# Funnel attention and gated FFN on one core: one beam search for the order of all visits, and column-tile groups of two pairs

## The chip, the cores and the metric

The kernel runs on one core of one Trainium2 chip. The metric is the device time of one execution in microseconds (us); the time of a kernel is the median of several runs.

## The reference

Attention with pooled queries, followed by a multiplicative FFN. All heads have 64 dimensions; 8 batches, 8 heads, 1152 keys, 576 pooled queries.

```python
q_pool = q.reshape(B, H, S // 2, 2, D).mean(axis=3)          # 8, 8, 576, 64
scores = 1 / sqrt(D) * q_pool @ k.T                          # 8, 8, 576, 1152
attn = softmax(scores)
attn_out = attn @ v                                          # 8, 8, 576, 64
x = attn_out.transpose(0, 2, 1, 3).reshape(4608, 512)
a, b = x @ w1, x @ w2                                        # 4608, 1024
out = ((a * b) @ w3) @ w_out                                 # 4608, 512
```

## The kernel before

**Pairs, slots and visits.** Two heads are one pair (32 pairs, `NP`). For a pair, the 9 key tiles times 576 queries are one flat row of 5184 score columns, and the rows of all pairs follow one another. They are cut into 324 slots of 512 columns. A slot is a few matmuls (`scores`, L396, 64 rows of the array for each of the two heads) into one of three PSUM tiles `psc`, and one exponential on ScalarE (L401) into a ring `ring` in SBUF that holds 2.67 pairs. Three slots make a visit; there are 108 visits. A pair is 3.375 visits long.

**What stands between the scores.** After its three slots, a visit has a string of steps in an order that a planner writes down while the program is built:

- `A`, an AV group (`av_step`): attention weights times values for 128 queries of a pair, 18 matmuls (L426) over the 9 key tiles and two heads. A pair has four such tiles and one of the last 64 queries. There the two heads go to two column halves of the array (L423, 18 matmuls too, called `C` in this text). All write into one PSUM bank, `avb`. A ones column in the values gives the sums; VectorE takes the reciprocal (L452, L446), scales (L460, L448) and so makes `xbt` or `xb5`. Its transpose is done in the next `A` by one matmul on PE (`T`: L467, or L469 for the 64 queries) with a copy on VectorE (L476, L478); for pairs from 8 on (`XD`) the four 128-query tiles go by one DMA transpose instead (`x_dma`, L436, SyncE's queue).
- `f` and other filler steps (`fill`): products of w3 and w_out early on (turnings of w3 L496, products L505), then the FFN in chunks of 512 tokens: 16 projections (L527, 4 matmuls) and 4 output steps (L571, 8 matmuls, called `F`). A filler uses the single bank `mo`, or borrows a `psc` bank (the tile is then `mot`).
- `P`: transposes of keys and queries of pairs 1 to 7 on PE into a `psc` bank (`transp_pe`, L336). From pair 8 on a DMA transpose makes `kqT` (L328, SyncE's queue).

PE has three tilings: 64 rows by 128 columns for scores, 128 by 64 for `C`, 128 by 128 for all the rest.

**The planner.** `_Plan` keeps running times of PE, ScalarE, VectorE, the three `psc` banks, `mo` and `avb`. For each visit on its own, `visit` tries all strings of up to six steps, adds the next three slots, and takes the string of least cost: PE time lost, plus 0.2 x the distance from a set pace (`PACE` = 3.09 us a visit, kept in `due`), plus a price for a late `avb`, less a bonus for AV groups done. A chunk of the FFN comes into the queue when its AV groups are done, and, where its `x` comes by DMA, `HELD` = 5 groups later. After the last visit the remaining AV groups and steps alternate (the tail).

**Queues.** SyncE's queue carries, in program order, the loads of k, q and v, the `kqT` transposes and `x_dma`; GpSimd's queue carries the casts to 16 bits, early loads, and the stores of outputs from three `osb` buffers (L539). `prepare` issues casts and loads two pairs ahead.

Of the kernel before, what the change touches and what calls it, by code (L numbers as in the profile page):

```python
# [121 lines left out]
class _Plan:  # L122
# [3 lines left out]
    SWITCH, SLOT, AV, LAST, TURN, PAIR, SEEN = 0.09, 0.222, 0.553, 0.36, 0.055, 0.76, 0.05  # L126
    STEP = {0.5: 0.45, 1: 0.866, 2: 1.73}

    def __init__(self, t):
        self.t = t  # L130
        self.act = self.mo = self.av = self.dve = 0.0
        self.psc = [0.0, 0.0, 0.0]
        self.k = 0
        self.mode = "row"

    def _pe(self, mode, free, took):
        if mode != self.mode:
            self.t += self.SWITCH
            self.mode = mode
        self.t = max(self.t, free) + took  # L140
# [5 lines left out]
    def scores(self):  # L146
        b = self._psc()
        self._pe("row", self.psc[b] + self.SEEN, self.SLOT)
        self.act = max(self.act, self.t + 0.21) + 0.953
        self.psc[b] = self.act + 0.07  # L150

    def fill(self, n, at, scored):
        b = self._psc() if scored else None
        self._pe("full", max(at, (self.psc[b] if scored else self.mo) + self.SEEN), self.STEP[n])
        self.dve = max(self.dve, self.t + 0.2) + 0.69
        if scored:
            self.psc[b] = self.dve + 0.07
        else:
            self.mo = self.dve + 0.07

    def av_group(self, turns, last):
        if last:
            self._pe("col", self.av + self.SEEN, self.LAST)
        else:
            self._pe("full", self.av + self.SEEN, self.AV)
        if turns:
            self._pe("full", 0.0, self.TURN)
        self.dve = max(self.dve, self.t + 0.2) + 0.49 + (0.21 if turns else 0.0)
        self.av = self.dve + 0.02

    def pair(self, at):
        b = self._psc()
        self._pe("full", max(at, self.psc[b] + self.SEEN), self.PAIR)
        self.dve = max(self.dve, self.t + 0.1) + 0.9
        self.psc[b] = self.dve + 0.07

    def copy(self):
        p = _Plan(self.t)
        p.__dict__.update(self.__dict__)
        p.psc = list(self.psc)  # L180
        return p

    def visit(self, due, turns, must, groups, pair_at, eager):


        best = [None, None]

        def end(p, seq, work, av):
            q = p.copy()
            for _ in range(3):  # L190
                q.scores()
            lost = q.t - self.t - work - 3 * self.SLOT
            cost = lost + 0.2 * abs(p.t - due) + 0.3 * max(q.av + self.SEEN - q.t, 0.0)
            cost -= eager * min(len(turns), 6) * av
            if best[0] is None or cost < best[0] - 1e-9:
                best[:] = [cost, seq]

        def step(p, seq, work, av, f, pr):
            if pr == len(pair_at) and av >= must:
                end(p, seq, work, av)  # L200
            if len(seq) > 5 or p.t > due + 0.5 and av >= must:
                return
            if pr < len(pair_at):
                q = p.copy()
                q.pair(pair_at[pr])
                step(q, seq + "P", work + self.PAIR, av, f, pr + 1)
            if av < min(len(turns), 3):
                q = p.copy()
                q.av_group(*turns[av])
                took = (self.LAST if turns[av][1] else self.AV) + (self.TURN if turns[av][0] else 0.0)  # L210
                step(q, seq + "A", work + took, av + 1, f, pr)
            if f < min(len(groups), 4):
                n, at = groups[f]
                for b in (False, True):
                    q = p.copy()
                    q.fill(n, at, b)
                    step(q, seq + "ms"[b], work + self.STEP[n], av, f + 1, pr)

        step(self, "", 0.0, 0, 0, 0)
        return best[1]  # L220


@with_exitstack
def kernel(
# [11 lines left out]
    nc = tc.nc  # L236
# [21 lines left out]
    NU = NP * NT5  # L258
# [23 lines left out]
    xps = avb[:, 448:448 + QT]  # L282
# [131 lines left out]
    def av_pair(i):  # L414
        p, t = i // NT5, i % NT5
        va = vaugs[p % NVA]
        o = (i % 3) * 2 * E1
        for jt in range(NJ):
            c0 = ((p * NJ + jt) * Sq) % RING + TO[t]
            for u in range(2):  # L420
                if t == QM:

                    nc.tensor.matmul(avb[u * QT:u * QT + QT, o:o + E1], ring[:, u, c0:c0 + QT], va[:, u, jt, :],  # L423
                                     start=(jt == 0), stop=(jt == NJ - 1), skip_group_check=True)
                    continue
                nc.tensor.matmul(avb[:, o + u * E1:o + u * E1 + E1], ring[:, u, c0:c0 + 128], va[:, u, jt, :],  # L426
                                 start=(jt == 0 and u == 0), stop=(jt == NJ - 1), skip_group_check=True)
# [11 lines left out]
    def on_pe(i):  # L439
        return i >= 0 and (i // NT5 < XD or i % NT5 == QM)  # L440

    def av_norm(i):
        o = (i % 3) * 2 * E1
        if i % NT5 == QM:

            nc.vector.reciprocal(out=rzall[:, i, :], in_=avb[:, o + D:o + E1].to_broadcast([128, 2]))  # L446
            xbts[i] = att.tile([128, 2, D], FP16, tag="xbt", bufs=3, name="xbt")
            nc.vector.scalar_tensor_tensor(out=xbts[i], in0=avb[:, o:o + D].unsqueeze(1).to_broadcast([128, 2, D]),  # L448
                                           scalar=rzall[:, i, 0:1], in1=half, op0=ALU.mult, op1=ALU.mult)
            return  # L450
        av = avb[:, o:o + 2 * E1].rearrange("p (u e) -> p u e", e=E1)
        nc.vector.reciprocal(out=rzall[:, i, :], in_=av[:, :, D:E1].rearrange("p u o -> p (u o)"))  # L452
        p, t = i // NT5, i % NT5
        if i // NT5 < XD:
# [9 lines left out]
    def x_turn(i):  # L464
        xb = xbts.pop(i).rearrange("p u d -> p (u d)")
        if i % NT5 < QM:
            nc.tensor.transpose(xpt, xb, ident16)  # L467
        else:
            nc.tensor.matmul(xps, xb, both, start=True, stop=True, skip_group_check=True)  # L469

    def x_copy(i):
        p, t = i // NT5, i % NT5
# [4 lines left out]
        else:  # L477
            nc.vector.tensor_copy(out=xT[:, hp, c0:c0 + QT], in_=xps)  # L478
# [133 lines left out]
    def fill(scored=False):  # L612
# [3 lines left out]
        if not tail[0]:  # L616
            plan.fill(n, at, scored)
# [58 lines left out]
    pair_end = [((p + 1) * FLAT - 1) // G // VS for p in range(NP)]  # L676
    done_at = {}
    for c in range(B * Sq // CH):
        last = max((b * HP + HP - 1) * NT5 + t for b in range(B) for t in range(NT5)
                   if xpos(b, t) < (c + 1) * CH and xpos(b, t) + (128 if t < QM else QT) > c * CH)  # L680
        done_at.setdefault(last, []).append(c)

    final.extend(done_at[max(done_at)])
    plan = _Plan(7.0)
    PACE = 3.09
    W3_AT, WO_AT, KQ_AT = (17.5, 28.0, 35.0, 44.0), 20.5, {2: 24.5}
    avn = [0]
    ready, held = [], []
    HELD = 5

    def av_step():
        i = avn[0]
        avn[0] += 1
        av_pair(i)
# [5 lines left out]
        if i >= XD * NT5 and i % NT5 == QM - 1:  # L700
            x_dma(i // NT5)
        if i:
            for c in done_at.get(i - 1, []):
                held.append((i + (HELD if i > XD * NT5 else 0), c))
        while held and held[0][0] <= i:
            ready.append(held.pop(0)[1])

    NVIS = NS // VS
    seen, due, started = -1, 0.0, False
    for vis in range(NVIS):  # L710
        if vis == T_START:
            queue.append(t_groups())
        due = max(due + PACE, plan.t + 2.6)
        for s in range(vis * VS, vis * VS + VS):
# [13 lines left out]
            plan.scores()  # L728
# [5 lines left out]
        avail = NT5 * sum(1 for e in pair_end if e < vis) - avn[0]  # L734
        turn = [p for p in range(1, NPE) if (p * FLAT // G) // VS - 1 == vis]
        while ready:
            started = True
            queue.append(moe_groups(ready.pop(0)))
        head(4)

        must = sum(1 for i in range(avn[0], min(avn[0] + avail, NU))
                   if ((i // NT5 * NJ * Sq + RING + TO[i % NT5]) // G) // VS <= vis + 1)
        for what in plan.visit(due, [(on_pe(avn[0] + j - 1), (avn[0] + j) % NT5 == QM) for j in range(avail)], must, [(g[0], g[3]) for g in ahead],
                               [KQ_AT.get(p, 0.0) for p in turn], 0.05 if started else 0.1):
            if what == "P":
                plan.pair(KQ_AT.get(turn[0], 0.0))
                transp_pe(turn.pop(0))
            elif what == "A":
                av_step()
                plan.av_group(on_pe(avn[0] - 2), (avn[0] - 1) % NT5 == QM)  # L750
            else:
                fill(what == "s")
    fill(True)
    while avn[0] < NU:
        av_step()
        while ready:
            queue.append(moe_groups(ready.pop(0)))
        fill(True)
    tail[0] = True
    x_turn(NU - 1)  # L760
    x_copy(NU - 1)
    ready.extend([c for _, c in held] + done_at.get(NU - 1, []))
    while ready:
        queue.append(moe_groups(ready.pop(0)))
# [57 lines left out]
```

## Time and profile before

| | us |
|---|---|
| median of 3 runs | 420.6 (419.92 to 420.74) |
| profiled execution, time | 421.74 |
| profiled execution, span | 419.7 |
| PE busy | 404.0 |
| ScalarE (ACT) busy | 325.8 |
| VectorE (DVE) busy | 207.1 |
| scores from / tail from | 7.13 / 345.6 |

The span runs from the first to the last instruction; the time of an execution has 2.04 us more around it. The granted PE clock is 0.997 on the mean. Matmuls overlap in the pipeline and their ends are modelled, so distances between starts say more than bars.

### The profile page before, as it was taken

What the parts mean: (1) busy time and instruction counts of PE and PEld (TensorE: products, weight loads), DVE (VectorE), ACT (ScalarE), POOL (GpSimd) and SP (SyncE); (2) the same over time, 40 slices, a digit from 0 to 9 for tenths busy, and PEclk for the clock granted to TensorE, in tenths of its full rate; (3) what the DMA queues carried; (4) which work ended last, traced back from release to release, by engine and by line L of the source; (5) the groups of instructions that cost most, each with busy time, mean ns of one, the idle gap of its engine ahead of it and who ended that gap; (6) DMA issues with size and microseconds to landing.
All of it is one profiled execution on the core that took longest, in us unless ns stands there. A gap on an engine that the chain in (4) does not pass through costs nothing.

```text
span 419.7 us, 12781 instructions
## 1 busy us (share of the span) xinstructions
PE 404.0 (96%) x5337; PEld 246.6 (59%) x5337; DVE 207.1 (49%) x601; ACT 325.8 (78%) x359; POOL 166.8 (40%) x210
## 2 busy tenths in 40 slices
PE   3899999999999999999999999999999999999995
PEld 1577886555566655655566556565577755444442
DVE  1255665664445534555455534555354546624231
ACT  4888879889999898989899889998999882223231
POOL 5879876360751427412564428141652011000000
PEclk9999999999999999999999999999999999999998
DMA  8999999999795999989989999899995323020203
GB/s 261 264 299 287 254 299 318 321 240 261 160 262 140 256 265 247 279 175 256 329 202 246 266 244 280 167 258 274 256 235 117 59 64 64 14 101 2 100 0 106
DMA packets 90960, 86.34 MB, mean 206 GB/s; under 512 B 59664, under 2 KB 64272, under 8 KB 90896
## 3 DMA queue, kind: packets, MB, share of 16 engines
q1 hardware_dynamic: 81600, 59.32, 59.7%
q0 software_dynamic: 8720, 25.10, 20.8%
q10 hardware_dynamic: 576, 1.05, 0.7%
q8 instruction: 42, 0.69, 0.7%
q14 instruction: 22, 0.18, 0.2%
HBM read 67.11 MB, written 9.44 MB: 182 GB/s over the span
## 4 chain that ended last, share of the span: by engine, by line
PE 89%; ACT 4%; DMA 3%; DVE 2%; issue 1%; POOL 0%; ACTq 0%; DVEq 0%
PE psc L396 19%; PE avb L426 17%; PE mot L527 16%; PE mo L527 14%; PE mo L571 9%; PE mot L571 5%; ACT ring L401 3%; PE mo L505 3%; PE avb L423 3%; DMA out_dram<-osb 2%; PE ptk L336 2%; DMA qst<-in_q_dram 1%; PE mo L496 1%; PE avb L467 1%; DVE kqT L338 1%
## 5 line engine op out<-in xcount | busy, mean ns | idle before, releaser
L401 ACT ACTIVATE ring<-psc 128x1024 f16<-128x1024 f32 x324 | 307.5, 1026 | 34.4 <-PE psc L396 33.4
L396 PE MATMUL psc<-kqT 64*128 64x512 f16 (+7 forms) x1152 | 97.9, 292 | 3.4 <-ACT ring L401 0.9
L426 PEld LDWEIGHTS <-ring 128*128 128x128 f16 x2304 | 83.2, 98 | 27.2 <-issue 8.5
L426 PE MATMUL avb<-vaug,ring 128*128 128x65 f16 x2304 | 91.5, 194 | 1.1 <-DVE xT L478 0.9
L308 POOL CAST kq<-kst 128x1152 f16<-128x1152 f32 x31 | 35.7, 1151 | 79.3 <-DMA kqT<-kq 64.7
L396 PEld LDWEIGHTS <-kqT 64*128 64x128 f16 x1152 | 46.1, 95 | 34.9 <-issue 12.7
L571 PE MATMUL mo<-T,gT 128*128 128x512 f16 x192 | 45.5, 380 | 0.0
L527 PEld LDWEIGHTS <-w2sb 128*128 128x128 f16 x320 | 28.0, 97 | 27.4 <-issue 3.7
L571 PEld LDWEIGHTS <-gT 128*128 128x128 f16 x280 | 25.5, 98 | 30.6 <-issue 3.1
L527 PEld LDWEIGHTS <-w1sb 128*128 128x128 f16 x320 | 28.1, 97 | 25.6 <-issue 1.8
L539 POOL DMA_DIRECT2D out_dram<-osb x21 | 11.7, 555 | 76.3 <-DVE osb L581 41.1
L452 DVE RECIPROCAL rzall<-avb 128x2 f32<-128x2 f32 x128 | 21.1, 165 | 41.5 <-PE avb L426 22.4
L527 PE MATMUL mot<-xT,w1sb 128*128 128x512 f16 (+2 forms) x176 | 41.1, 360 | 0.0
L312 POOL TENSOR_TENSOR kq<-qst 128x512 f16<-128x512 f32 x31 | 39.4, 1272 | 1.3 <-DMA qst<-in_q_dram 1.3
L321 POOL CAST vaug<-vst 128x1152 f16<-128x1152 f32 x32 | 36.6, 1143 | 8.3 <-DMA vst<-in_v_dram 8.2
L560 DVE TENSOR_TENSOR gT<-mo,asb 128x512 f16<-128x512 f32 x36 | 24.9, 692 | 25.9 <-PE mo L527 25.9
L527 PE MATMUL mo<-xT,w2sb 128*128 128x512 f16 (+2 forms) x176 | 37.2, 341 | 0.0
L527 PE MATMUL mot<-xT,w2sb 128*128 128x512 f16 x144 | 37.0, 379 | 0.2 <-ACT ring L401 0.2
L581 DVE TENSOR_SCALAR osb<-mo 128x512 f32<-128x512 f32 x24 | 16.6, 692 | 41.1 <-PE mo L571 38.0
L560 DVE TENSOR_TENSOR gT<-mot,asb 128x512 f16<-128x512 f32 x36 | 24.9, 692 | 23.3 <-PE mot L527 23.3
L554 ACT COPY asb<-mot 128x512 f32<-128x512 f32 x20 | 11.7, 585 | 31.2 <-PE mot L527 31.2
L527 PE MATMUL mo<-xT,w1sb 128*128 128x512 f16 (+2 forms) x144 | 33.0, 356 | 0.0
(76 smaller groups left out, 314.9 us busy)
## 6 DMA issues: line engine op xcount, KB each, us to landing
vst<-in_v_dram SPq DMA_DIRECT2D x25, 576.0 KB, 5.1
kst<-in_k_dram SPq DMA_DIRECT2D x23, 576.0 KB, 5.9
qst<-in_q_dram SPq DMA_DIRECT2D x23, 512.0 KB, 7.7
out_dram<-osb POOLq DMA_DIRECT2D x21, 256.0 KB, 6.1
kst<-in_k_dram POOLq DMA_DIRECT2D x8, 576.0 KB, 9.1
qst<-in_q_dram POOLq DMA_DIRECT2D x8, 512.0 KB, 10.0
vst<-in_v_dram POOLq DMA_DIRECT2D x7, 576.0 KB, 7.5
out_dram<-osb SPq DMA_DIRECT2D x9, 256.0 KB, 2.1
```

The lines of the kernel that those rows point to most:

```text
L308: nc.gpsimd.tensor_copy(out=kq16[:, 0:NJ].rearrange("p c u d -> p u c d"), in_=kst.rearrange("p u (c d) -> p u c d", d=D))
L312: eng.tensor_tensor(out=kq16[:, NJ:NJ + QM].rearrange("p c u d -> p u c d"), in0=qv[:, :, :, 0], in1=qv[:, :, :, 1], op=ALU.add)
L321: nc.gpsimd.tensor_copy(out=va[:, :, :, 0:D], in_=vs.pop(p).rearrange("p u (c d) -> p u c d", d=D))
L396: nc.tensor.matmul(psc[:, u, f - s * G:f - s * G + ln], kT2[u * 64:u * 64 + 64, jt, :], qpT[u * 64:u * 64 + 64, i0:i0 + ln], start=True, s ...
L401: nc.scalar.activation(out=ring[:, :, r0:r0 + G], in_=psc, func=AF.Exp, bias=0.0, scale=SCALE)
L423: nc.tensor.matmul(avb[u * QT:u * QT + QT, o:o + E1], ring[:, u, c0:c0 + QT], va[:, u, jt, :], start=(jt == 0), stop=(jt == NJ - 1), skip_ ...
L426: nc.tensor.matmul(avb[:, o + u * E1:o + u * E1 + E1], ring[:, u, c0:c0 + 128], va[:, u, jt, :], start=(jt == 0 and u == 0), stop=(jt == N ...
L452: nc.vector.reciprocal(out=rzall[:, i, :], in_=av[:, :, D:E1].rearrange("p u o -> p (u o)"))
L527: nc.tensor.matmul(pw[:, d0:d0 + n], wt[:, mc, ft * 128:ft * 128 + 128], xT[:, mc, a:a + n], start=(mc == 0 and d0 == 0), stop=(mc == NC - ...
L560: nc.vector.tensor_tensor(out=t["g"][:, ft, :], in0=pb, in1=t["a"], op=ALU.mult)
L571: nc.tensor.matmul(po, t["g"][:, ft, tt:tt + 128], T16[:, ft, :], start=(ft == 0), stop=(ft == NF - 1))
L581: nc.vector.tensor_scalar_mul(out=osb, in0=po, scalar1=1.0 / (SCL * SCL))
```

## The change

One function, `_visits`, plans all visits before any is recorded. It keeps a beam of plans for each count of AV groups and filler steps done (`width` = 3 for each, none more than `REACH` = 1.5 worse than the best), extends each by all strings of up to five steps or 2.3 us, and returns the strings of the plan that loses least PE time at the end. There is no pace and no bonus. Some prices of `_Plan` are set anew, and its waits for `psc`, `mo` and `avb` include `SEEN`.

The 64-query groups of two pairs become one group of 36 matmuls with two results side by side in `avb`, one reciprocal, two scalings, two matmuls for the transposes and one copy. The order of AV groups becomes: four tiles of an even pair, the common 64-query group, four tiles of the odd pair (`UNITS`; 144 groups instead of 160). `avb` has two result slots instead of three. A chunk is released four groups (`HELD` = 4) after the last group whose DMA transpose it reads. The last group of all is now a 128-query group of pair 31.

```diff
-    SWITCH, SLOT, AV, LAST, TURN, PAIR, SEEN = 0.09, 0.222, 0.553, 0.36, 0.055, 0.76, 0.05
+    SWITCH, SLOT, AV, LAST, TURN, PAIR, SEEN = 0.097, 0.222, 0.556, 0.285, 0.057, 0.77, 0.05
...
-    def visit(self, due, turns, must, groups, pair_at, eager):
...
+def _visits(n, start, units, pairs, fills, free, ready, width):
+    p = _Plan(7.0)
+    for _ in range(3):
+        p.scores(0.0)
+    beam = {(0, 0): [p]}
+    for vis in range(n):
...
+        def end(p, seq, na, f):
+            q = p.copy()
+            for _ in range(3 if vis + 1 < n else 0):
+                q.scores(ready[vis + 1])
+            q.past = (p.past, seq)
+            cost = q.lost() + 0.3 * max(q.av - q.t, 0.0) + 0.15 * max(q.mo - q.t, 0.0)
+            new.setdefault((na, f), []).append((cost, seq, q))
...
+        floor = min(x[0] for v in new.values() for x in v)
+        beam = {}
+        for key, v in sorted(new.items()):
+            v.sort(key=lambda x: x[:2])
+            v = [x[2] for x in v[:width] if x[0] < floor + REACH]
+            if v:
+                beam[key] = v
...
-    NU = NP * NT5
+    UNITS = [x for p in range(0, NP, 2) for x in
+             [(p, t) for t in range(QM)] + [(p + 1, QM)] + [(p + 1, t) for t in range(QM)]]
+    NU = len(UNITS)
...
-    xps = avb[:, 448:448 + QT]
+    xps = avb[:, 384:384 + 2 * QT]
...
+    def av_mm(i):
+        p, t = UNITS[i]
+        o = (i % 2) * 2 * E1
+        for pp in ((p - 1, p) if t == QM else (p,)):
+            va = vaugs[pp % NVA]
+            for jt in range(NJ):
+                c0 = ((pp * NJ + jt) * Sq) % RING + TO[t]
+                for u in range(2):
+                    if t == QM:
+                        nc.tensor.matmul(avb[u * QT:u * QT + QT, o:o + E1], ring[:, u, c0:c0 + QT], va[:, u, jt, :],
+                                         start=(jt == 0 and pp != p), stop=(jt == NJ - 1), skip_group_check=True)
...
+            o += E1
...
+        if t == QM:
+            xbts[i] = att.tile([128, 2, 2, D], FP16, tag="xbc", bufs=2, name="xbc")
+            for n in range(2):
+                nc.vector.scalar_tensor_tensor(out=xbts[i][:, n], in0=av[:, n, 0:D].unsqueeze(1).to_broadcast([128, 2, D]),
+                                               scalar=rzall[:, i, n:n + 1], in1=half, op0=ALU.mult, op1=ALU.mult)
+            return
...
+            for n in range(2):
+                nc.tensor.matmul(xps[:, n * QT:n * QT + QT], xb[:, n].rearrange("p u d -> p (u d)"), both,
+                                 start=True, stop=True, skip_group_check=True)
...
-    PACE = 3.09
...
-    HELD = 5
+    HELD = 4
...
+                    n = max(n, i + 2, index[(p, QM - 1)] + 1 + HELD if p >= XD and t < QM else 0)
+        loose.setdefault(min(n, NU + 1), []).append(c)
...
+    order = _visits(NVIS, T_START, units, {v: [KQ_AT.get(p, 0.0) for p in ps] for v, ps in turn.items()},
+                    fills, free, [0.0] * (NVIS + 1), 3)
...
-        due = max(due + PACE, plan.t + 2.6)
...
+        for what in order[vis]:
             if what == "P":
-                plan.pair(KQ_AT.get(turn[0], 0.0))
-                transp_pe(turn.pop(0))
+                transp_pe(turn[vis].pop(0))
             elif what == "A":
                 av_step()
...
```

## The prediction

> **What bounds the kernel now.** I read the page first: busy shares, then the chain that ended last.
>
> ```profile
> PE 404.0 (96%) x5337; PEld 246.6 (59%) x5337; DVE 207.1 (49%) x601; ACT 325.8 (78%) x359; POOL 166.8 (40%) x210
> ...
> PE 89%; ACT 4%; DMA 3%; DVE 2%; issue 1%; POOL 0%; ACTq 0%; DVEq 0%
> ```
>
> TensorE (PE) carries the time. But "96% busy" does not say that only 4% can be won: a matmul's end is modelled, so short waits vanish inside its bar. The next view is therefore the timeline of PE over two visits, read by starts alone.
>
> ```profile
> 126.78 0.71 PE L426 MATMUL avb<-vaug,ring 128*128 128x65 f16 x18
> 127.42 0.83 PE L396 MATMUL psc<-kqT 64*128 64x192 f16 x12
> 128.19 1.04 PE L527 MATMUL mo<-xT,w2sb 128*128 128x512 f16 x4
> 129.06 1.03 PE L527 MATMUL mot<-xT,w1sb 128*128 128x512 f16 x4
> 130.02 0.48 PE L423 MATMUL avb<-vaug,ring 128*64 128x65 f16 x18
> 130.43 1.01 PE L396 MATMUL psc<-kqT 64*128 64x384 f16 x10
> 131.37 0.72 PE L426 MATMUL avb<-vaug,ring 128*128 128x65 f16 x18
> 131.93 0.19 PE L469 MATMUL avb<-both,xbt 128*128 128x64 f16 x1
> 131.96 1.02 PE L527 MATMUL mo<-xT,w2sb 128*128 128x512 f16 x4
> 132.84 0.71 PE L426 MATMUL avb<-vaug,ring 128*128 128x65 f16 x18
> 133.47 0.83 PE L396 MATMUL psc<-kqT 64*128 64x512 f16 x10
> ```
>
> The columns are start, length, then the work. Three things are to be seen. (a) An AV group (L426) takes 0.64 us when scores follow (126.78 to 127.42) and 0.56 when another 128x128 matmul follows (131.37 to 131.93). Over all groups the medians are 644 and 548 ns: a change of the array's tiling costs 97 ns; the step L527 shows the same (957 against 862). (b) Three slots of scores take 0.76 normally (128.19 - 127.42), but 0.94 at 130.43: 0.18 us of waiting that no "idle" entry reports. (c) The visit that starts at 127.42 is 3.01 us long. What PE waited for is ScalarE's exponentials:
>
> ```profile
> 233.86 2.85 ACT L401 ACTIVATE ring<-psc 128x1024 f16<-128x1024 f32 x3 [0.29 <-PE psc L396]
> ```
>
> Three exponentials need 2.85 us and empty the three `psc` banks one after another. A visit that is too short meets a bank that is still full. The trace gives the shortest lengths: after a visit of 2.71 us with no filler in a `psc` bank the scores were stretched by 0.25, after one of 2.82 by 0.14, so 2.96 us is enough; after 3.01 us with one borrowed bank (L527 into `mot`) by 0.18, so 3.18-3.19 is enough.
>
> Adding up, over the PE timeline, all start-to-start times above these normal ones from visit 4 (20.41 us) to the end gives 9.6 us. 0.95 of it is one DMA wait:
>
> ```profile
> 162.38 0.69 DVE L581 TENSOR_SCALAR osb<-mo 128x512 f32<-128x512 f32 x1 [3.05 <-DMA out_dram<-osb]
> ...
> 163.52 0.48 PE L423 MATMUL avb<-vaug,ring 128*64 128x65 f16 x18 [0.88 <-DVE xb L460]
> ```
>
> VectorE waited for an output store to free `osb`, the AV result behind it was late, and PE stood. The other 8.6 us come from the order of the visits, which is what the change replaces.
>
> **Part by part, from the built order of both kernels.**
>
> *Tiling changes.* The old order has 32 column-tile groups and 255 changes of tiling mode, the new one 16 and 235. 20 x 0.097 = **-1.9 us**, all on the path.
>
> *Merged groups.* An old group has 18 matmuls in 285 ns from first to last start (16.8 ns apart) and 415 ns to the next mode, so 318 without the change of mode. A group of 36 is not in the trace. At the same spacing it takes 35 x 16.8 + 33 = 620 ns against 2 x 318: 16 x -0.016 = **-0.3 us**. Upper bound: the second half at the spacing of L426 (530 / 17 = 31 ns), 18 x 14 ns = +0.25 us each, +4.0 us in all. Below -0.3 there is nothing, since the same columns are streamed. I take -0.3, because the nearest row is the same instruction.
>
> [...] The trace sides with 16.8 ns so far, although its weight-load row is longer for L423 (110 ns) than for L426 (98 ns).
>
> *VectorE's share.* Two old groups cost it 2 x (0.166 + 0.351 + 0.214) us, a merged one 0.166 + 2 x 0.351 + 0.214: 0.38 us less, 16 times, hidden: VectorE is 49% busy. In one place it isn't: where `C, step, A` stand together (4 visits) the next AV group waits for `avb` behind about 1.1 us of VectorE work with 0.96 us of PE work above it: +0.1 to 0.2 each, +0.5. Two result slots in `avb` instead of three cost nothing: already now an AV group waits for VectorE's last access to this bank (visit 32, 0.88 us, two groups in a row), so the third slot bought no overlap.
>
> *The order.* I wrote down each visit's length from the rows above (scores 0.66, AV 0.55, C 0.32 or 0.62, step 0.865, output step 1.73, each change 0.097) and compared with 2.96 or 3.18. Old, visits 4 to 106: 15 of `A f A` (2.82), 8 of `A T f A` (2.84), 8 of `C f A T` (2.71), 10 of `f f C` (3.00), 9 of `f f A` (3.13), a lone output step (2.58), `A T A` (1.98), small shortages in visits 4 to 26, and 0.6 us of borrowed banks asked for sooner than 1.5 us after the visit began. Sum 11.0 us, against 8.6 measured, so the rule overstates by a factor 0.79. New: 14 of `A f A`, 24 of `f f A`, no `C f A T`, no `A T A`, no lone output step; 4.8 us, and 1.0 for early banks (visits 4, 5, 6, 15, 22, 47). 5.8 x 0.79 = 4.6, with the 0.5 from above 5.1. Difference **-3.5 us** from 8.6; ends: 3.0 us of waits left (-5.6) or none of it gained (0).
>
> *Start.* Visit 3 swaps two turnings of w3 between banks. They run 107 ns per transpose there, twice the later 55, and the order does not change that: 0.
>
> *Queues.* On SyncE's queue each `kqT` transpose stands behind an `xb` transpose (`x_dma`) that waits for an AV group. In the old order that group lay 3.3 to 6 visits before the pair's first scores, in the new one 4.7 to 6.7 (once 3.3). Slack from landing to first use was 2.2 to 13 us already, so this gains nothing. GpSimd's stores and casts keep their kinds and numbers. The one store wait of 0.95 us came in one of six runs of three or four output steps, 3.14 us apart, which the new order has too, elsewhere against the loads; I count half of it as gone, **-0.5 us**.
>
> *Tail.* After the last scores PE has only steps in both, 863 ns apart without a gap, and the checks at the end are as before: 0. GpSimd and DMA have no other new work.
>
> Sum: -1.9 - 0.3 - 3.5 - 0.5 = -6.2 us. The profiled execution has a span of 419.7 and a time of 421.74, so 415.5; it lies 1.1 above the median of the runs (420.6). Forecast **414.4 us**.
>
> **Rivals.**
>
> *Data late for a chunk (418.0 us).* A chunk's first step now is released four groups after the last AV group whose transpose it reads, before it was five to seven. For the chunks at visits 47, 61, 75 and 89 that leaves three visits of 3.14 plus scores and a group, 10.8 us. In the trace, AV end to landing of `xT` took 3 to 6 us mostly, but 9.4 to 11.7 for five of 24, all around output stages; the new order puts these four into an output stage. Up to 0.9 us each (11.7 - 10.8) is 3.6: 418.0 us. For it: those five. Against: they were issued late behind loads that waited for GpSimd's casts, which in the new order stand ahead of these stages. [...]
>
> *Waits only move (418.4 us).* If 24 visits at 3.13 us turn out as costly as the short ones they replace, only -2.2 remains.
>
> *The long column group is bound by weight loads (418.6 us).* The +4.0 of above.
>
> *Slower: `kqT` transposes (424 us).* In and after output stages they took 9.6 to 12 us from issue to landing (pairs 11, 15, 16, 19, 24, 29), elsewhere 4. The tight ones are issued 7.3 us before use. A slow transpose that is also tight makes scores wait 12 - 7.3 = 4.7 us, and ScalarE with them; two such pairs cost 9.4 and outweigh 6.2: about 424. It decides once late landings sum to over 6 us. DMA is near full (share 0.94 from 127 to 346 us) and the pace rises by 2%. Against it: the slow ones had slack of 2.5 to 7 us, and the new queue order loosens most of the tight ones.
>
> That the order isn't the stated one is excluded by the built order.
>
> **How the numbers follow.** Forecast, 412 to 416.5: 0.66. Data late: 0.13. Waits move: 0.07. Weight loads: 0.05. Slower: 0.09. The lower end is -1.9 - 0.3 - 5.6 - 0.95 = -8.8: 411.8. The upper end takes in the first three rivals: 418.6. A measurement can tell about 0.2%, 0.8 us. Faster 0.88, same 0.04, slower 0.08.
>
> **What would show it.** Right: group of 36 near 0.62 us without the mode change; 235 changes; scores mostly 0.76 us, no stretch over 0.3 after visit 10; waits from visit 4 about 5 to 6 us. Wrong: PE steps at visits 47, 61, 75, 89 waiting for a DMA; scores waiting for `kqT`; spacing in the column group over 20 ns.

## The result, and the profile after

| | before | changed |
|---|---|---|
| median, us | 420.67 (419.92 to 421.26, 4 runs) | 415.36 (415.13 to 416.02, 4 runs) |
| ratio, 95% interval | | 0.9877 [0.9858, 0.9897] |
| profiled execution, time / span, us | 421.74 / 419.7 | 416.02 / 414.1 |

The changed kernel is 5.3 us (1.2%) faster; 6.2 us and 414.4 us were forecast. A ratio here compares a kernel with the kernel before, run beside it. Ratios use fast runs alone, and of all runs in this document one is slow: the one of 430.2 us without a hold. The page of the changed kernel, the same two lines as before:

```profile
PE 399.9 (97%) x5337; PEld 246.9 (60%) x5337; DVE 205.5 (50%) x573; ACT 323.4 (78%) x353; POOL 167.6 (40%) x212
...
PE 93%; ACT 2%; DMA 2%; DVE 1%; issue 1%; SPq 0%; POOL 0%; ACTq 0%
```

The bound is the same and its share of the chain rose from 89 to 93%. PE has as many matmuls as before (5337). The timeline of PE shows where the time came from (start, length, work):

```profile
128.26 0.83 PE L431 MATMUL psc<-kqT 64*128 64x192 f16 x12
129.02 1.04 PE L566 MATMUL mo<-xT,w2sb 128*128 128x512 f16 x4
129.90 1.03 PE L566 MATMUL mot<-xT,w1sb 128*128 128x512 f16 x4
130.76 0.71 PE L462 MATMUL avb<-vaug,ring 128*128 128x65 f16 x18
131.40 0.87 PE L431 MATMUL psc<-kqT 64*128 64x384 f16 x10
132.21 0.72 PE L462 MATMUL avb<-vaug,ring 128*128 128x65 f16 x18
132.77 1.02 PE L566 MATMUL mo<-xT,w2sb 128*128 128x512 f16 x4
133.63 0.71 PE L462 MATMUL avb<-vaug,ring 128*128 128x65 f16 x18
134.27 0.93 PE L431 MATMUL psc<-kqT 64*128 64x512 f16 x10
135.13 0.72 PE L462 MATMUL avb<-vaug,ring 128*128 128x65 f16 x18
...
140.92 0.77 PE L459 MATMUL avb<-vaug,ring 128*64 128x65 f16 x36
141.63 1.04 PE L566 MATMUL mo<-xT,w1sb 128*128 128x512 f16 x4
142.61 0.71 PE L462 MATMUL avb<-vaug,ring 128*128 128x65 f16 x18
```

The visit at 128.26 (`f f A`) is 3.14 us long and its successor's scores take 0.81 instead of 0.76: the 0.05 that was priced. The visit at 131.40 (`A f A`) is 2.87 long and is followed by scores of 0.86 (134.27 to 135.13). The group of 36 takes 0.705 us to the next tiling on the median of all 16, that is 0.608 without the 0.097, with starts 576 ns from first to last: 16.5 ns apart. The step behind it takes 0.98 instead of 0.87, because the AV group after it waits 0.11 for `avb`.

Spans of the two profiled executions, added up in the same way (us):

| | before | changed | difference | forecast |
|---|---|---|---|---|
| tiling changes, 255 and 235, at 0.097 | 24.7 | 22.8 | -1.9 | -1.9 |
| 64-query groups, 32 x 0.318 and 16 x 0.608 | 10.2 | 9.7 | -0.45 | -0.3 |
| PE's waits from visit 4 on, but for the next line | 8.7 | 5.9 | -2.8 | -3.5 |
| wait for an output store | 0.95 | 0 | -0.95 | -0.5 |
| visits 0 to 3, start of visit 4 | 20.41 | 20.72 | +0.3 | 0 |
| last step's start to the end | 6.50 | 6.67 | +0.2 | 0 |
| span | 419.7 | 414.1 | -5.6 | -6.2 |

Two of the rows may belong to these executions more than to the change. The kernel before with half exponentials, further down, has the same order of PE and the same instructions in visits 0 to 3; in its profile there is no wait for an output store, and visit 4 starts at 19.43 us instead of 20.41.

### The profile page after: what moved, and what is told of

It reads as the page before. It is cut to its first block, busy times and chain, and to the rows that moved or that the text cites. A ratio compares the mean times of both kernels' runs of the same rounds, so it can differ in the third digit from the quotient of the medians.

```text
span 414.1 us, 12744 instructions
## 1 busy us (share of the span) xinstructions
PE 399.9 (97%) x5337; PEld 246.9 (60%) x5337; DVE 205.5 (50%) x573; ACT 323.4 (78%) x353; POOL 167.6 (40%) x212
## 3 DMA queue, kind: packets, MB, share of 16 engines
q10 hardware_dynamic: 576, 1.05, 0.8%
## 4 chain that ended last, share of the span: by engine, by line
PE 93%; ACT 2%; DMA 2%; DVE 1%; issue 1%; SPq 0%; POOL 0%; ACTq 0%
PE psc L431 20%; PE avb L462 17%; PE mot L566 16%; PE mo L566 15%; PE mo L610 11%; PE mot L610 5%; PE mo L544 3%; PE avb L459 3%; ACT ring L436 2%; PE ptk L371 2%; DMA kst<-in_k_dram 2%; DVE kqT L373 1%; PE mot L544 1%; PE mo L535 1%; PE mot L535 1%
## 5 line engine op out<-in xcount | busy, mean ns | idle before, releaser
L462 PEld LDWEIGHTS <-ring 128*128 128x128 f16 x2304 | 84.4, 98 | 26.3 <-issue 7.1
L431 PE MATMUL psc<-kqT 64*128 64x512 f16 (+7 forms) x1152 | 96.2, 291 | 3.4 <-ACT ring L436 0.9
L578 POOL DMA_DIRECT2D out_dram<-osb x23 | 12.7, 551 | 101.6 <-DVE rzall L483 99.9
L483 DVE RECIPROCAL rzall<-avb 128x2 f32<-128x2 f32 x144 | 23.8, 165 | 37.0 <-PE avb L462 20.2
L566 PE MATMUL mot<-xT,w2sb 128*128 128x512 f16 (+2 forms) x156 | 38.0, 368 | 0.0
L566 PE MATMUL mo<-xT,w2sb 128*128 128x512 f16 (+2 forms) x164 | 36.2, 349 | 0.0
L595 DVE COPY asb<-mo 128x512 f32<-128x512 f32 x32 | 22.1, 691 | 24.0 <-PE mo L566 23.7
```

What stands on the lines that cost most here:

```text
L431: nc.tensor.matmul(psc[:, u, f - s * G:f - s * G + ln], kT2[u * 64:u * 64 + 64, jt, :], qpT[u * 64:u * 64 + 64, i0:i0 + ln], start=True, s ...
L566: nc.tensor.matmul(pw[:, d0:d0 + n], wt[:, mc, ft * 128:ft * 128 + 128], xT[:, mc, a:a + n], start=(mc == 0 and d0 == 0), stop=(mc == NC - ...
L595: nc.vector.tensor_copy(out=t["a"], in_=pa)
```

## The experiments

Two theories stood against each other first. Mine: the search saves waits and tiling changes, the merged groups save tiling changes, and the two add up. The rival: the merged groups carry the gain because they relieve VectorE and the bank `avb`.

**Search alone.** The groups are left single; two slots in `avb` and the hold of four groups stay as in the changed kernel, so no run separates these from the search:

```diff
-    UNITS = [x for p in range(0, NP, 2) for x in
-             [(p, t) for t in range(QM)] + [(p + 1, QM)] + [(p + 1, t) for t in range(QM)]]
+    UNITS = [(p, t) for p in range(NP) for t in range(NT5)]
...
-        for pp in ((p - 1, p) if t == QM else (p,)):
+        for pp in (p,):
```

> The beam search alone: 64-query groups stay one per pair (160 AV groups), two result slots, release after four groups. Built order: 256 changes of tiling (old 255, changed kernel 235); visits too short for ScalarE by 4.35 us in all by the rule of shortest lengths (old 9.5, changed 4.35). Theory (waits on psc and tiling changes add up): the changed kernel's 415.4 plus 21 x 0.097 plus 16 x 0.028 = 417.9 us. Rival (the merged groups carry the gain, by relieving VectorE and avb): near the kernel before, 420 us.

Measured 420.2 us, ratio 1.0005 [0.9994, 1.0017]: at first sight the rival. But the waits within the visits had fallen as the theory says, to 5.1 us with the tail's left out. What ate the gain stood in the tail: the last group of all was now the 64-query group which two chunks wait for, so both were released at the very end, and the remaining AV groups followed one another with no step between them (2.2 us of waits for `avb`), as PE's timeline shows:

```profile
367.00 0.71 PE L461 MATMUL avb<-vaug,ring 128*128 128x65 f16 x18
368.35 0.71 PE L461 MATMUL avb<-vaug,ring 128*128 128x65 f16 x18 [0.63 <-DVE xb L495]
369.64 0.48 PE L458 MATMUL avb<-vaug,ring 128*64 128x65 f16 x18 [0.58 <-DVE xb L495]
370.77 0.20 PE L504 MATMUL avb<-both,xbt 128*128 128x64 f16 x1 [0.65 <-DVE xbt L484]
```

The end was 0.8 us longer than the changed kernel's too. So the tail was mended, with the visits left as they were:

```diff
-    UNITS = [(p, t) for p in range(NP) for t in range(NT5)]
+    UNITS = [(p, t) for p in range(NP) for t in (range(NT5) if p < NP - 1 else (QM, 0, 1, 2, 3))]
```

> The beam search alone, as in e1_search_split, but the last pair's 64-query group stands before its four tiles, so that the chunk before the last is released in time and no two AV groups follow each other in the tail; the order of the 108 visits is the one of e1_search_split. Theory (the search gains its waits without the merged groups; e1_search_split lost 2.2 us of waits between bare AV groups in the tail and 1 us at its end): 420.2 - 3 = 417.2 us, that is the changed kernel plus 21 tiling changes (2.0 us) and 0.45 us for shorter groups, less 0.5 us of waits. Rival (the search brings nothing without the merged groups): 420 us.

Measured 417.99 us, ratio 0.9942 [0.9923, 0.9961], 0.8 us above the expectation. The search alone gains 2.3 us. The changed kernel is 2.6 us better; 21 tiling changes and the shorter groups make 2.5 us of that.

**Merged groups alone**, with the old planner's rules (pace, bonus, one visit at a time) for the 144 groups:

```diff
-    order = _visits(NVIS, T_START, units, {v: [KQ_AT.get(p, 0.0) for p in ps] for v, ps in turn.items()},
-                    fills, free, [0.0] * (NVIS + 1), 3)
+    order = _greedy(NVIS, T_START, units, {v: [KQ_AT.get(p, 0.0) for p in ps] for v, ps in turn.items()}, fills, free)
```

> The merged groups alone: the visit-by-visit planner with its pace plans the 144 groups, everything else as in the changed kernel. Built order: 234 changes of tiling, visits too short by 11.2 us by the rule (old 9.5). Theory: 420.7 - 21 x 0.097 - 0.45 + 0.8 x 1.7 = 419.6 us. Rival (the merged groups carry the gain): 416 us.

Measured 423.39 us, ratio 1.0078 [1.0061, 1.0095]: slower than both expectations. The 21 changes of tiling are saved, but the waits from visit 4 on are 14.7 us. In the changed shape an even pair's four groups become ready together and then a pair and a half pass until the next ones; the old planner puts two AV groups in a row (timeline of PE):

```profile
156.56 0.72 PE L458 MATMUL avb<-vaug,ring 128*128 128x65 f16 x18
158.07 0.72 PE L458 MATMUL avb<-vaug,ring 128*128 128x65 f16 x18 [0.79 <-DVE xb L493]
```

1.51 us from start to start instead of 0.55. There are five such places, three with nothing between the groups and two with only a transpose, and they cost 4.1 us; the kernel before has one, of 0.88. That is 3.3 of the 5.1 us by which the waits grew. The rest was not taken apart. So the parts do not add up: merging is worth -2.6 us under the search and, with the two slots and the hold of four, +3.2 us under the old planner.

**Is it the lookahead or the dropped pace?** A beam that keeps only plans level with the best:

```diff
-REACH = 1.5
+REACH = 1e-6
```

> The changed kernel with a beam that keeps only the plans level with the best after each visit (REACH 1e-6 instead of 1.5): no pace and no bonus, but no look ahead either. Built order: 235 tiling changes, visits too short by 8.0 us by the rule (changed kernel 4.35, old planner with merged groups 11.2). Theory (lookahead carries the part of the waits that the removal of the pace does not): 415.4 + 0.8 x 3.7 = 418.3 us, with AV groups in pairs waiting for avb as in e2_old_planner_merged. Rival (it was the pace that cost, not the missing lookahead): 415.5 us.

Measured 426.85 us, ratio 1.0149 [1.0126, 1.0173], 8.5 us more than my own expectation. The rule of shortest visits knows only `psc`; the waits are at `avb` (PE's waits, in total, times, longest):

```profile
PE avb L462 <- DVE xb L497: 5.9, 10, 0.6
PE avb L462 <- DVE xT L515: 1.4, 2, 0.7
PE avb L459 <- DVE xb L497: 1.3, 2, 0.6
```

Without lookahead AV groups pile up until two or three must stand in one visit. Lookahead is worth 11.5 us here. The old planner looks no further, yet with its pace and bonus it comes to 423.39 us on the same groups, 3.5 less; they seem to have been a rough stand-in for lookahead. This is not shown apart, for some of its prices differ too.

**Whose waits are they?** The exponentials are halved, in both kernels, with PE's order untouched. These kernels leave out half of that work and serve as a test only:

```diff
-        nc.scalar.activation(out=ring[:, :, r0:r0 + G], in_=psc, func=AF.Exp, bias=0.0, scale=SCALE)
+        ge = G if s < RING // G else G // 2
+        nc.scalar.activation(out=ring[:, :, r0:r0 + ge], in_=psc[:, :, 0:ge], func=AF.Exp, bias=0.0, scale=SCALE)
```

> The kernel before with each exponential, after the first 27 slots, on half of its columns (the other half of the ring keeps older values); the order of PE is the same to the instruction. Theory (the waits of 8.6 us are ScalarE's hold on psc): all but those of the first visits and the store wait go, 7 us, so 413.7 us, and scores take 0.76 us everywhere. Rival (PE waits for VectorE, DMA or its own pipeline): 420.5 us, stretched scores as before.

Measured 415.85 us, ratio 0.9903 [0.9889, 0.9917]: 4.3 us less, not 7. The waits from visit 4 on go from 9.6 to 4.8 us. The store wait of 0.95 is not among the 4.8, and 0.7 of them is new: the scores of visit 97 wait for a `kqT` transpose. So of the 8.7 us that were put down to the order of the visits, 4.1 stay. The scores of 0.94 us that the prediction showed first are still 0.91 (timeline of the kernel with half exponentials):

```profile
127.32 0.48 PE L424 MATMUL avb<-vaug,ring 128*64 128x65 f16 x18
127.73 0.83 PE L396 MATMUL psc<-kqT 64*128 64x384 f16 x10
128.03 0.16 DVE L447 RECIPROCAL rzall<-avb 128x2 f32<-128x2 f32 x1
128.23 1.57 ACT L402 ACTIVATE ring<-psc 128x512 f16<-128x512 f32 x3 [1.43 <-PE psc L396]
128.23 0.35 DVE L449 SCALAR_TENSOR_TENSOR xbt<-avb,rzall,half 128x128 f16<-128x128 f32 x1
128.64 0.72 PE L427 MATMUL avb<-vaug,ring 128*128 128x65 f16 x18
```

ScalarE is idle for 1.43 us, the scores run through, and yet the AV group starts 0.15 us late: VectorE is done with the 64-query group only at 128.58. Where a visit ends with `C` and the next begins with `A`, two waits lie over each other, and ScalarE's was not the only one.

> The changed kernel with each exponential, after the first 27 slots, on half of its columns; the order of PE is the same. Theory: of its 5.9 us of waits about 3 are ScalarE's, so 412.3 us; waits for kqT in visits 10, 13 and 20 (0.35 us each) and for avb behind a merged group (0.11 us, four times) stay. It should lie only about 1.5 us below the kernel before with half exponentials, for tiling changes and shorter groups are all that is left, less the kqT waits. Rival: 415.4 us.

Measured 413.06 us, ratio 0.9821 [0.9806, 0.9835], 2.3 us less; 0.8 us above the expectation, and 2.8 below the kernel before with half exponentials, where 1.5 was expected. Of these 1.3 us more, the new wait for `kqT` in the other kernel makes 0.7 in its profile; the rest is open. In this kernel too a wait had come up that the changed kernel does not have. The profile is of the longest of its four runs, 414.63 us; the others took 411.9 to 413.53, so what this wait makes of the 0.8 us is not known. PE's timeline of the changed kernel:

```profile
203.45 0.72 PE L462 MATMUL avb<-vaug,ring 128*128 128x65 f16 x18
204.01 1.02 PE L566 MATMUL mo<-xT,w1sb 128*128 128x512 f16 x4
204.97 0.77 PE L459 MATMUL avb<-vaug,ring 128*64 128x65 f16 x36
```

and of the one with half exponentials, which is ahead by some 2.5 us there:

```profile
201.46 0.81 PE L567 MATMUL mo<-xT,w1sb 128*128 128x512 f16 x3
204.45 0.38 PE L567 MATMUL mo<-xT,w1sb 128*128 128x512 f16 x1 [2.18 <-DMA xT<-xb]
```

It is the chunk of visit 61: its first step reads the transpose of pair 15, which landed at 204.40 with half exponentials and at 204.51 in the changed kernel, where the matmul that reads it starts at 204.66. In this execution the rival "data late for a chunk" stood 0.15 us away.

**How near is that rival?** The hold of a chunk after its last DMA group, 4 in the changed kernel, set to 0 and to 6:

> The changed kernel with a chunk released right after the last AV group whose DMA transpose it reads (hold 0 instead of 4; the search plans again, 233 tiling changes, visits too short by 3.76 us by the rule instead of 4.35). In the changed kernel the transposes of pairs 11, 15, 19 and 23 land 5 to 10 us after their AV group. Theory (data late is a real bound, and the hold pays for it): the first step of the chunk at visit 45 stands right behind the group and waits some 5 us, those at visits 60, 74 and 88 stand 10 us behind and wait 0 to 2 us; 420 us. Rival (a landing is early enough in any case): 415 us.

> The changed kernel with a chunk released six groups after the last one whose DMA transpose it reads (hold 6 instead of 4). Built order: 235 tiling changes, visits too short by 6.16 us by the rule (4.35). Theory: no wait for xT, but the search has fewer steps to place: 0.8 x 1.8 = 1.5 us more, 416.9 us. Rival (in the changed kernel data is late unseen, and a longer hold helps): under 415 us.

Hold 0: 427.83 us (423.64 to 430.2), ratio 1.014 [1.0097, 1.0182], nearer the theory than the rival but 7.8 us above it. In the profile, which is of the run of 430.2 us, PE waits 3.7 us for `xT` in visit 45 and 6.4 in visit 60, where 5 and 0 to 2 were expected, and then runs slowly for some microseconds (last section). Hold 6: 416.36 us, ratio 0.9918 [0.9897, 0.994]; 1.0 us above the changed kernel, where 1.5 was expected. Its waits are 7.3 instead of 5.9 us; but 0.95 of them is a wait of visit 6 for VectorE's copies into `kqT`, in an execution in which visit 4 began 1.6 us earlier, so the sum alone does not show that fewer steps to place are the cause. A hold of four is thus enough in the changed kernel, and its margin is no constant: in the two kernels of the next part, with a hold of four as well, the transpose of pair 15 landed 8.6 and 1.1 us ahead of its first use.

> The kernel of e10_hold_six with each exponential, after the first 27 slots, on half of its columns. In e4_after_half_exp one chunk start waited 2.2 us for a DMA transpose, which hid part of the gain. Theory (without that wait the ScalarE part of the waits shows): 6.16 x 0.8 = 4.9 us less than e10_hold_six, less 1 us that sits at VectorE, so 413 us; no wait for xT. Rival: the DMA wait comes back and the time stays above 414 us.

Measured 413.29 us, ratio 0.984 [0.9823, 0.9857]; 3.1 us below e10_hold_six, and no wait for `xT`. Waits from visit 4 on go from 7.3 to 4.2 us. ScalarE's share is again less than the rule gives (3.1 for 4.9 less 1).

**Can the rest be planned away?**

```diff
-        turn.setdefault((p * FLAT // G) // VS - 1, []).append(p)
+        turn.setdefault((p * FLAT // G) // VS - (2 if p in (3, 4, 6) else 1), []).append(p)
```

> The changed kernel with the transposes of keys and queries of pairs 3, 4 and 6 planned one visit earlier. In the changed kernel the scores of visits 10, 13 and 20 wait 0.35 us each for VectorE's last copy into kqT; the planner has no price for this. Theory (these waits are real time and not only moved): 1.0 us less than the changed kernel, 414.4 us. Rival (the wait moves to ScalarE's bank, since visits 9, 12 and 19 are followed by the same three slots): 415.4 us.

```diff
-        self._put(b, self._dve(0.1, 0.95))
+        self._put(b, self._dve(0.2, 1.2) + 0.05)
...
-        self.av = self._dve(0.2, 0.45 + 0.2 * (last == 2) + (0.2 if turns else 0.0))
+        self.av = self._dve(0.2, 0.45 + 0.4 * (last == 2) + (0.2 if turns else 0.0))
```

> The changed kernel with two prices of its planner mended from the trace: a key transpose holds its psc bank for VectorE's three copies of 1.2 us (was 0.95), and a merged group's scaling takes VectorE 0.2 us more. Built order: 234 tiling changes, visits too short by 4.44 us by the rule (4.35). Theory (the 1.0 us of waits for kqT and 0.45 us for avb behind merged groups can be planned away): 414.0 us. Rival (as in e6_keys_early they only move to another visit): 415.4 us.

Measured 415.34 and 415.65 us (ratios 0.988 [0.986, 0.9901] and 0.9893 [0.9878, 0.9907]), no different from the changed kernel's 415.36: the rival in both. With the keys turned earlier the wait of 0.34 us reappears in visits 9 and 23, again for VectorE's copies out of the `psc` bank of a key transpose (three copies, 1.22 us, in visit 9 of the changed kernel). With the prices mended, PE waits some 0.2 us ahead of the transposes of visits 9 and 12, as the changed kernel does ahead of those of visits 15 and 22, and for ScalarE ahead of filler steps (1.4 us in all instead of 0.3); the sum of the waits stays at 6.2 us. Neither version beats the changed kernel.

## Why the prediction was right, point by point

*The bound and the mechanism.* PE's path set the time, and it fell by what its order saved. Forecast 414.4, measured 415.36, within the range and with the sign. That the sum came out so near is in part luck: the store wait gave 0.45 us more than forecast, and may be of one execution only, while the waits within the visits gave 0.7 less.

*Tiling changes.* 20 fewer in the built order, and the price holds in the changed kernel: AV groups take 644 ns ahead of scores and mostly 544 to 561 otherwise.

*Merged groups.* -0.45 us for -0.3, at 16.5 ns a matmul instead of 16.8; so -0.3 was no floor. The weight-load row for the column tiles is 110 ns as before, and 36 in a row run as fast as 18. The rival of the weight loads, which took 31 ns a matmul for the second half, is out.

*VectorE behind a merged group.* Forecast 0.1 to 0.2 us in four visits; measured 0.11 in visits 41, 48, 54 and 68.

*The order: the term that was mis-sized.* -2.8 us instead of -3.5. The step that failed is the reading that what PE waited for is ScalarE's exponentials, from which the two shortest lengths were taken. Halving ScalarE's work left 4.1 us of the old order's 8.7 us of waits, and 3.4 of the changed one's 5.9 (5.7 less the 2.3 for `xT`). ScalarE's share was about half; most of the rest is VectorE's hold on `avb` (0.15 us at `C` then `A`, 0.88 at `A T A`) and on the bank of a key transpose. The rule counted the first kind under the wrong owner: the length of 3.18 was read from the very scores at 130.43 whose wait stayed. That its sum came near all the same is luck. For the second kind it had no price: visits 10, 13 and 20 wait 0.34 to 0.37 us each, 1.05 in all, where the old order has one such wait of 0.34 (visit 6). So the sign "no stretch over 0.3 after visit 10" failed. The forecast waits of 5.1 us came out as 5.9.

*Queues.* The store wait did not recur: 0.95 us for 0.5. `kqT` landed 3.0 to 12.3 us ahead of its use (2.2 to 13 before), so the rival on the slower side had no place here. It came up once, in the kernel before with half exponentials (0.7 us). The prediction's "elsewhere 4" for its landing was too smooth: in the trace before, the other transposes took 3.9 to 8.2 us.

*Start and end.* +0.3 and +0.2 us, forecast at nothing, in single executions. The start of visit 4 alone differs by 1 us or more between executions of the same first visits: 20.41 and 19.43 with the kernel before and its version with half exponentials, 20.72 and 19.51 with the changed one and its version.

*The rivals.* "Waits only move" was wrong as a whole and right for what was left (keys turned earlier, prices mended). "Data late" didn't happen, by 0.15 us in one of four chunks. Its price of 3.6 us for a hold of four was not tested. Without a hold two chunks waited 10.1 us in the profiled run, which took 14.8 us more than the changed kernel's median (12.5 on the median of its four runs); that the late data cost more than its waits there had no place in the price.

## What to carry to other kernels

Read PE's waits from starts, since bars with modelled ends hide them (0.18 us at 130.43 had no idle entry); then find each wait's owner by making that owner faster, because two waits that lie over each other look like one (of these 0.18 us, 0.15 stayed with half exponentials). A plan that looks one step ahead can be worse than the order it replaces when a change of shape makes work ready in bursts: test the parts apart and together. A hold that covers a DMA's landing should be checked by its slack in the traces of several runs (0.15, 1.1 and 8.6 us for pair 15 here), not by the absence of a wait in one.

## What the runs showed of the hardware

In the kernel without a hold PE stood for 3.7 us (155.39 to 159.07) and for 6.4 us (207.50 to 213.92), and its granted clock was at half when it went on. The windows of that profile (start:end, length, busy time of PE, PEld, DVE, ACT and POOL, granted clock, DMA share, GB/s), ahead of the first gap, behind it, later, and about the second gap:

```profile
150.00:154.00 4.00, 4.00 (x47) 1.95 (x46) 1.79 (x4) 3.43 (x5) 3.04 (x4) 1.00 0.97 315
159.00:162.00 3.00, 2.93 (x32) 1.88 (x32) 1.16 (x3) 0.70 (x1) 0.83 (x1) 0.50 1.09 248
162.00:165.00 3.00, 3.00 (x32) 1.88 (x31) 0.57 (x3) 2.15 (x3) 3.00 (x4) 0.52 1.03 382
165.00:168.00 3.00, 3.00 (x37) 1.61 (x34) 1.67 (x4) 2.09 (x3) 0.04 (x1) 1.00 0.18 60
210.00:214.00 4.00, 0.08 (x1) 0.08 (x1) 0.00 (x0) 0.00 (x0) 0.94 (x1) 0.84 1.28 195
214.00:217.00 3.00, 3.00 (x23) 1.62 (x22) 1.38 (x2) 0.00 (x0) 1.46 (x2) 0.50 1.12 344
217.00:220.00 3.00, 3.00 (x37) 1.99 (x35) 0.71 (x4) 2.15 (x3) 2.42 (x3) 0.58 0.83 307
```

The granted clock is 1.00 from 150 to 154 and 0.50 from 159 to 162 us. If it is 0.50 or 1.00 at each time, my estimate from the means of 0.52, 0.84 and 0.58 is that it came back at 164.9 us, fell again at 212.7, 5.2 us into the second gap, and came back at 219.5. PE was working for 5.8 and 5.6 us of these stretches, and what it did took up to twice as long (a step 1.71 us at 214.30 instead of 0.86, scores 1.39 us at 217.14 instead of 0.76). My estimate from this is some 5.7 us lost behind 10.1 us of waits, in a run that is 14.8 us above the changed kernel's median. The amount differs from run to run: the other three took 423.64, 427.52 and 428.13 us, at mean granted clocks of 0.994, 0.990 and 0.982.
